# Cached attention and a Mish block on one core: the first and the last value loads cut differently, and half of the weights turned ahead of a wait

## The chip, the core and the metric

The kernel runs on one core of one Trainium2 chip. The core's engines are named as in the profile: PE (TensorE, matrix products), DVE (VectorE), ACT (ScalarE), POOL (GpSimd) and SP (SyncE, which here only issues loads). Sixteen DMA engines move data between the chip's memory and SBUF. The metric is the device time of one execution in microseconds (us); the time of a kernel is the median of its runs.

## The reference

One decode step, all in float32: 8 sequences, one new token each, model width 512.

- `xn = layernorm(x)`.
- Attention: `q = xn @ wq` gives 32 query heads of width 128. There are 8 key and value heads, each shared by 4 query heads, and a cache of 8192 positions: `scores = q k^T / sqrt(128)`, softmax over the 8192 positions, then the weighted sum of the values, then `@ wo`.
- A dense block: `h = xn @ w1 + b1` (1792 wide), `h * tanh(softplus(h))` (Mish), then `@ w2`.
- Result: `x + attention + dense block`, 8 x 512 numbers.

The key cache and the value cache hold 8 x 8 x 8192 x 128 numbers each, 268 MB each. Every number of them is used once, so some 561 MB pass from memory to the core in one execution.

## The kernel before, in words

**Units and packs.** The work on the caches is cut into 32 *units* (`UNITS`); a unit is two heads of one sequence: 8192 KB of keys (K0 to K31) and 8192 KB of values (V0 to V31). Two units make a *pack* (`PACKS` = 16), which share one softmax pass.

**Buffers.** SBUF has room for one unit of keys and one unit of values only. `kvb` (64 KB in each of 128 partitions) holds keys, `kva` (the same size) holds values, `kvw` (16 KB a partition) holds a quarter of `wq` or `wo`. At the beginning `kva` holds `w1`; at the end `kvb` holds the last unit's values and then `w2`.

**The loads** are all issued by SP, in the order of `early_loads` and `later_loads`, on one queue whose transfers land in order. A load that writes a buffer in use waits on SP until that buffer is told free, and everything behind it in the list waits with it. `k_free` is told by ACT when a unit's scores are done (line 729 of the program, `scalar_program`); `v_free` is told by DVE when a unit's values are done (`pass_on(s.valued, s.v_free)`), the first one when the products with `w1` are done; `w_free` is told by DVE in `keep_queries` and `add_outputs`. The order at the start is: wq0, K0, w1, wq1, K1, the first three quarters of V0 (semaphore `v0_in`), K2, the last quarter of V0 (`v_in`; it waits for `v0_in`), K3, wq2, V1, K4, V2, K5, wq3, V3, and so on, with a part of `wo` behind K9, K17 and K25. The order at the end is: K31, V29, the first 5/8 of V31 into `kvb` (`va_in`), V30, the last 3/8 of V31 (`vb_in`), then w2 in four parts (`w2a_in` to `w2d_in`) with the last part of `wo` behind the first. The first part of w2 waits for `w2_free`, told by PE when it has used the first 5 of 8 rounds of V31.

**PE** (`tensor_program`) runs a loop over n from -1 to 32. In step n it does the scores of unit n, on odd steps the sums that bring a pack's scores together (`rows`), sometimes a quarter of the queries (`queries`), then the values of unit n-2 (`values`, in 8 rounds over the buffer, `ROUNDS`), and on odd steps `merges`; `turn` and `outputs` follow when a head pair is complete. Ahead of the loop `turn_x` turns the normalised x twice: whole, for the queries, and, after POOL has sorted it (`x_split`), in eight parts for the products with `w1` (`mish_products`, in step 0). Behind the loop it does the end: the rest of V31, the early products with `w2` (`down_early`), `merges`, `turn`, `outputs`, and the rest of the products with `w2` (`down`), with `add_up` between them.

**ACT** copies scores out of PSUM and computes exponentials, in two halves of a pack's positions (`exponents(0)`, `exponents(1)`; the second half needs `exp_next`, which DVE tells when it has turned the first).

**DVE** (`vector_program`) does, for each pack: `expand` (it spreads the queries of a unit), `gather(0)` of the pack before, `maximum`, `expand`, then waits for the values of the pack's second predecessor unit (`valued`), passes that on as `v_free`, and does `gather(1)` and `collect`. Then it turns both halves of the exponentials (`turn_exponents`: a transpose and an addition) and writes them as weights into `pt` (`weights(c, b)`: half c, unit b of the pack, two additions each). `pt[:, 0]` is what PE reads; `pt[:, 1]` is copied over it when the first unit's values are done. When all is written DVE tells `p_is`, on which PE's values wait.

Of the kernel before, what the change touches and what calls it, by code (L numbers as in the profile page):

```python
# [13 lines left out]
P = 128  # L14
B = 8
D = 512
# [7 lines left out]
G = 4  # L24
# [3 lines left out]
BW = 1024  # L28
# [4 lines left out]
Q = P // G  # L33
# [68 lines left out]
def kernel(  # L102
# [18 lines left out]
    def bank(shape, name):  # L121
        return nc.alloc_psum_tensor(name, list(shape), F32).ap()

    names = (
        "x_in b1_in k_in v_in w_in w1_in v0_in va_in vb_in w2_free w2a_in w2b_in w2c_in w2d_in "
        "k_free v_free w_free q_free c_free scored copied_ex "
        "x_ready x_pool x_turned x_split x_split_turned x_is xw_is id_pe id_dve root rooted "
        "q_is rows_are max_is max_turned max_wide max_back shifts_are exp_done exp_next "
# [74 lines left out]
    def load(landed, dst, src, free=None, n=0):  # L203
        got = sp.dma_start(dst, src)
        if n:
            got.wait_op(free, n, "sem-ge")
        got.then_inc(landed, 16)
        return got
# [7 lines left out]
    def load_v(n):  # L216
        given["v"] += 1
        return load(s.v_in, kva, unit(v, n), s.v_free, given["v"])
# [5 lines left out]
    def load_wq(i):  # L224
        return load_w(wq[i * CC : (i + 1) * CC])
# [4 lines left out]
    w1_sb = kva[:, : W1R * F // 2]  # L230
    w2_sb = kvb[:, : W2N * D]
    W2_PARTS = ((0, 8), (8, 11), (11, 13), (13, 14))
    FIRST_V = 3 * KR * BW // 4
    LAST_ROUNDS = 5
    LAST_V = LAST_ROUNDS * KR * BW // ROUNDS

    def early_loads():
        first = [act.dma_start(x_sb, x), load_wq(0), act.dma_start(b1_sb, b1.rearrange("(g f) -> g f", g=G))]
# [6 lines left out]
    def later_loads():  # L245
        load_wq(1)
        load_k(1)
        first = unit(v, 0)
        given["v"] += 1
        load(s.v0_in, kva[:, :FIRST_V], first[:, :FIRST_V], s.v_free, given["v"])  # L250
        for n in range(2, UNITS):
            load_k(n)
            p, b = divmod(n, PB)
            if b == 1 and p in (1, 2):
                load_wq(p + 1)
            if b == 1 and p in (4, 8, 12):
                load_wo(p // 4 - 1)
            if n == 2:
                load(s.v_in, kva[:, FIRST_V:], first[:, FIRST_V:], s.v0_in, 16)
            else:  # L260
                load_v(n - 2)
        last = unit(v, UNITS - 1)
        load(s.va_in, kvb[:, :LAST_V], last[:, :LAST_V], s.k_free, given["k"])
        load_v(UNITS - 2)
        load(s.vb_in, kvb[:, LAST_V:], last[:, LAST_V:], s.k_free, given["k"])
        parts = list(zip(W2_PARTS, (s.w2a_in, s.w2b_in, s.w2c_in, s.w2d_in)))
        for (lo, hi), landed in parts:
            cols = slice(lo * D, hi * D)
            load(landed, w2_sb[:, cols], rows_of(w2)[:, cols], s.w2_free, 1)
            if lo == 0:  # L270
                load_wo(PAIRS - 1)

    def pool_setup():
        scratch = pt.rearrange("p b c m t e h -> p (b c m t e h)")
# [24 lines left out]
        pool.close()  # L299

    def normalise():
        dve.memset(xnT, 0.0)
# [79 lines left out]

    def turn_x():
        scratch = pt.rearrange("p b c m t e h -> p (b c m t e h)")
        xc, xs = scratch[:B, :D], scratch[:B, 2 * D : 2 * D + W1R * P]
# [4 lines left out]
        last.then_inc(s.x_turned, 1)  # L390
        take(pe, s.x_split)
        for r in range(W1R):
            last = pe.transpose(O[:, r * B : (r + 1) * B], xs[:, r * P : (r + 1) * P], ident[:B, :B])
        last.then_inc(s.x_split_turned, 1)
# [312 lines left out]
    def add_up():  # L707

        for g in range(G):
            pe.matmul(X[Q * g : Q * g + B, :P], rsel[:, :B], acc[:, g * P : (g + 1) * P], start=False, stop=False)  # L710

    def part(e, value):

        return e.If_eq(e.to_reg(value), 0)
# [27 lines left out]
    def vector_program():  # L742
# [8 lines left out]
        with e.Fori(0, PACKS) as p:  # L751
            dve.take(s.q_free)
            expand(2 * p + 1)
            dve.close()
            with part(e, (p - 1) & 16):
                dve.pass_on(s.valued, s.v_free)
                gather(0)
                dve.tensor_copy(
                    pt[:, 0].rearrange("p c m t e h -> p (c m t e h)"),
                    pt[:, 1].rearrange("p c m t e h -> p (c m t e h)"),  # L760
                )
                dve.tell(s.p_is)
                dve.close()
            e.end_ifs()
            maximum()
            dve.take(s.q_free)
            expand((2 * p + 2) & (UNITS - 1))
            dve.close()
            with part(e, (p - 1) & 16):
                dve.pass_on(s.valued, s.v_free)  # L770
                gather(1)
                dve.tell(s.o_is)
                collect((p - 1) & (NP - 1))
                dve.close()
            e.end_ifs()
            with part(e, (p - 4) & 19):
                keep_turned()
                dve.close()
            e.end_ifs()
            turn_exponents(0)  # L780
            weights(0, 0)
            weights(0, 1)
            turn_exponents(1)
            weights(1, 0)
            weights(1, 1)
            row_sums()
# [23 lines left out]
    def tensor_program():  # L810
        turn_x()
        with pe.Fori(-1, UNITS + 1) as n:
            with part(pe, n & 32):
                scores()
            pe.end_ifs()
            with part(pe, n):
                mish_products()
            pe.end_ifs()
            with part(pe, (n - 1) & 33):
# [91 lines left out]
```

## Time and profile before

| | |
|---|---|
| time, median of 3 runs | 1317.35 us (1316.45 to 1317.71) |
| the profiled execution's own time | 1317.75 us |
| its span, first to last instruction | 1316.4 us |
| busy: PE, DVE, ACT | 705.9, 386.6, 146.1 us |
| moved by DMA | 561.17 MB, mean 426 GB/s |
| mean granted clock of PE | 0.761 |

The profile is one execution. Busy times overlap, since the engines run side by side; a wait is shown as idle time in front of an instruction, with what ended it (PEq or DVEq is the engine's own sequencer, waiting for a semaphore). Line 72 (`L72`) is the helper through which all of DVE's and POOL's work is recorded, so their rows are told apart by tiles: `os` is a gather, `raw<-wide` a turning of exponentials, `pt<-raw` weights, `wide<-h` the first operation of `keep_queries`, `qT<-qc` an expansion. Line 204 is the helper that issues loads. On PE, L449 is scores, L540 values, L393 the transposes of the sorted x, L563 merges, L581 turn, L608 outputs. In a timeline row the columns are start, duration, engine, line, operation, written and read tiles with shapes, count, and in brackets the idle time ahead of it. In a row of stretches the columns are the stretch, its length, the busy time of PE, PEld (weight loads of PE), DVE, ACT and POOL with the count of instructions, the granted clock of PE, the DMA engines' busy share and GB/s.

### The profile page before, as it was taken

How to read it: one execution, taken by the hardware profiler on the slowest of the kernel's cores; microseconds unless marked ns; L12 is line 12 of the kernel's file. 1: busy time of each engine (PE TensorE's matmuls, PEld its weight loads, DVE VectorE, ACT ScalarE, POOL GpSimd, SP SyncE). 2: the span in 40 equal slices, each digit the busy share in tenths (PEclk: the TensorE clock that was granted, in tenths of full speed). 3: DMA queues.
4: the chain of work that ended last, by engine and by line, in shares of the span. 5: the costliest groups of instructions: out<-in, count | busy, mean ns of one | idle time of the engine just before them, and what ended most of it. 6: DMA issues, size and time to landing. Idle time of an engine off the chain costs nothing. (4 is left out here: it accounts for less than half of the span.)

```text
span 1316.4 us, 16643 instructions
## 1 busy us (share of the span) xinstructions
PE 705.9 (54%) x6808; PEld 226.2 (17%) x6808; DVE 386.6 (29%) x613; ACT 146.1 (11%) x339; POOL 4.9 (0%) x10
## 2 busy tenths in 40 slices
PE   3455745536546455646545555554744645554637
PEld 1111211212112111211112111111211211111112
DVE  4442151512315032141501414041141412304051
ACT  0020110101111020110201111010111101111010
POOL 0000000000000000000000000000000000000000
PEclk9777968768778777877768677777867768777768
DMA  9997999999999999999999999999999999999997
GB/s 401 423 425 317 460 414 446 414 446 446 414 446 414 446 446 414 446 416 444 446 414 446 416 444 446 414 446 420 440 446 414 446 420 440 446 414 446 432 426 307
DMA packets 11551, 561.17 MB, mean 426 GB/s; under 512 B 1292, under 2 KB 1424, under 8 KB 1816
## 3 DMA queue, kind: packets, MB, share of 16 engines
q1 hardware_dynamic: 11520, 561.06, 98.8%
q8 instruction: 4, 0.07, 0.0%
q10 hardware_dynamic: 24, 0.02, 0.0%
q14 instruction: 3, 0.02, 0.0%
HBM read 561.01 MB, written 0.07 MB: 426 GB/s over the span
## 5 line engine op out<-in xcount | busy, mean ns | idle before, releaser
L449 PE MATMUL c<-kvb,qT 64*32 64x512 f32 x4096 | 288.8, 723 | 283.1 <-PEq L98 283.1
L540 PE MATMUL o<-kva,pt 128*32 128x512 f32 x1984 | 275.4, 717 | 190.1 <-PEq L98 190.1
L449 PEld LDWEIGHTS c<-kvb,qT 64*32 64x32 f32 x4096 | 87.9, 127 | 479.4 <-issue 479.4
L540 PEld LDWEIGHTS o<-kva,pt 128*32 128x32 f32 x1984 | 77.9, 129 | 376.6 <-issue 376.6
L72 DVE TENSOR_SCALAR os<-o,isel 128x128 f32<-128x128 f32 x31 | 10.9, 351 | 434.9 <-DVEq L98 434.9
L72 DVE STREAM_TRANSPOSE raw<-wide 128x2048 f32<-128x2048 f32 x36 | 126.0, 3501 | 11.3 <-DVEq L98 10.7
L498 ACT ACTIVATE wide<-s,nms 128x512 f32<-128x512 f32 x128 | 86.2, 685 | 384.3 <-ACTq L98 384.3
L72 DVE TENSOR_REDUCE nm<-s 128x1 f32<-128x1024 f32 x16 | 19.6, 1225 | 356.2 <-DVEq L98 356.2
L733 ACT COPY sc<-c 128x512 f32<-128x512 f32 x64 | 34.4, 589 | 566.0 <-ACTq L98 565.9
L465 PE MATMUL s<-sc,csel 64*128 64x512 f32 x256 | 59.3, 602 | 24.0 <-ACT sc L733 24.0
L72 DVE TENSOR_TENSOR pt<-raw 64x256 f32<-64x256 f32 x128 | 53.7, 419 | 4.2
L72 DVE TENSOR_TENSOR raw<-raw 128x1024 f32<-128x1024 f32 x32 | 39.2, 1226 | 2.9
L733 ACT ACT_TABLE_LOAD x16 | 20.5, 1283 | 169.3 <-ACTq L98 169.3
L465 PEld LDWEIGHTS s<-sc,csel 64*128 64x128 f32 x256 | 23.4, 186 | 61.1 <-ACT sc L733 38.5
L72 DVE SCALAR_TENSOR_TENSOR os<-o,isel,os 128x128 f32<-128x128 f32 x93 | 32.6, 351 | 3.3
L72 DVE TENSOR_TENSOR qT<-qc,bsel 128x512 f32<-128x512 f32 x33 | 22.9, 693 | 28.4 <-DVEq L98 26.1
L563 PE MATMUL x<-hsel,os 128*128 128x8 f32 x64 | 9.9, 263 | 30.2 <-PEq L98 30.2
L498 ACT ACTIVATION_READ_ACCUMULATOR wide<-s,nms 128x1 f32 x128 | 26.0, 203 | 0.0
L402 PE MATMUL h<-kvw,xnT 128*64 128x512 f32 x64 | 22.7, 854 | 3.0 <-PEq L98 1.8
L540 PE MATMUL c<-kvb,pt 128*32 128x512 f32 x64 | 9.7, 763 | 15.3 <-PEq L98 15.3
L474 PE MATMUL m<-ident,nm 128*1 128x128 f32 x16 | 4.3, 269 | 24.6 <-PEq L98 24.6
L608 PE MATMUL h<-kvw,oW 128*8 128x512 f32 x64 | 14.2, 1036 | 5.9 <-PEq L98 5.9
(99 smaller groups left out, 154.4 us busy)
## 6 DMA issues: line engine op xcount, KB each, us to landing
kvw<-in_wq SPq DMA_DIRECT2D x4, 2048.0 KB, 22.8
kvw<-in_wo SPq DMA_DIRECT2D x4, 2048.0 KB, 33.1
kva<-in_v SPq DMA_DIRECT2D x1, 6144.0 KB, 34.1
kvb<-in_v SPq DMA_DIRECT2D x1, 5120.0 KB, 21.7
kva<-in_w SPq DMA_DIRECT2D x1, 3584.0 KB, 36.2
kvb<-in_v SPq DMA_DIRECT2D x1, 3072.0 KB, 28.8
kva<-in_v SPq DMA_DIRECT2D x1, 2048.0 KB, 24.9
kvb<-in_w SPq DMA_DIRECT2D x1, 2048.0 KB, 9.0
```

The costliest lines, as they stand in the source:

```text
L72: got = getattr(self.e, method)(*args, **kw)
L402: last = pe.matmul(H[HE * e : HE * (e + 1), :], xnT[:, r].rearrange("p g q -> p (g q)"), kvw[:, r * BW + e * D : r * BW + (e + 1) * D], st ...
L449: last = pe.matmul(C[e][Q * g : Q * (g + 1), :], t[rows, r], kvb[rows, r * BW + c * 512 : r * BW + (c + 1) * 512], start=(r < 2), stop=(r ...
L465: last = pe.matmul(S[:, c * 512 : (c + 1) * 512], csel[half_of, b, e].rearrange("p u b h -> p (u b h)"), sc[b][e][half_of, :], start=(b == ...
L474: pe.transpose(M[:1, 0:P], nm, ident).then_inc(s.max_turned, 1)
L498: last = act.activation(ex[:, :, k, :], S[:, c * 512 : (c + 1) * 512].rearrange("p (t f) -> p t f", t=HT), AF.Exp, bias=nms[:, k : k + 1], ...
L540: last = pe.matmul(to[Q * c : Q * (c + 1), :], pt[:, b, j % 2, j // 2].rearrange("p t e h -> p (t e h)"), vt[:, W4 * DH * j : W4 * DH * (j ...
L563: pe.matmul(X[:, at : at + 2 * REP], os[b], hsel, start=True, stop=True)
L608: last = pe.matmul(H[Q * r : Q * r + B, :], oW[:, r, h, :], kvw[:, at : at + D], start=(start and h == 0), stop=(h == 1))
L733: last = act.copy(sc[b][e], C[e])
```

## The change

1. *First values.* The first part of V0 is 5/8 of the unit, not 3/4; the second part is 3/8. The load of wq2 moves from behind K3 to directly behind the second part of V0, ahead of K3. (wq3 stays behind K5.)
2. *The last two units of values.* The first part of V31 is 11/16 of the unit, the second 5/16; PE still uses 5 of 8 rounds of it at first. V30 is loaded in two parts, the first 6 of 8 rounds (`v_in`) and the last 2 (`v2_in`). PE's `values` in the loop is cut in the same way for every unit, with a take of one credit (`v_more`) between the cuts. POOL gives 30 credits at the start, and the 31st when V30's second part has landed.
3. *Weights.* DVE turns the first half of the exponentials and writes `weights(0, 1)` ahead of its wait for `valued`, and `weights(0, 0)` behind it as before.
4. *split_x.* The eight transposes of the sorted x leave `turn_x` and stand in step 0 of PE's loop, behind the scores of unit 0 and ahead of `mish_products`.
5. *fill.* Behind the last `merges` and behind the last `turn`, PE does four products whose result nobody reads (into the scores' bank).

```diff
-    FIRST_V = 3 * KR * BW // 4
+    FIRST_V = 5 * KR * BW // 8
+    EARLY_ROUNDS = 6
+    EARLY_V = EARLY_ROUNDS * KR * BW // ROUNDS
     LAST_ROUNDS = 5
-    LAST_V = LAST_ROUNDS * KR * BW // ROUNDS
+    LAST_V = 11 * KR * BW // 16
...
         for n in range(2, UNITS):
             load_k(n)
             p, b = divmod(n, PB)
-            if b == 1 and p in (1, 2):
-                load_wq(p + 1)
+            if n == 2:
+                load(s.v_in, kva[:, FIRST_V:], first[:, FIRST_V:], s.v0_in, 16)
+            if n in (2, 5):
+                load_wq(n // 2 + 1)
             if b == 1 and p in (4, 8, 12):
                 load_wo(p // 4 - 1)
-            if n == 2:
-                load(s.v_in, kva[:, FIRST_V:], first[:, FIRST_V:], s.v0_in, 16)
-            else:
+            if n > 2:
                 load_v(n - 2)
...
         load(s.va_in, kvb[:, :LAST_V], last[:, :LAST_V], s.k_free, given["k"])
-        load_v(UNITS - 2)
+        given["v"] += 1
+        load(s.v_in, kva[:, :EARLY_V], early[:, :EARLY_V], s.v_free, given["v"])
+        load(s.v2_in, kva[:, EARLY_V:], early[:, EARLY_V:], s.v_free, given["v"])
         load(s.vb_in, kvb[:, LAST_V:], last[:, LAST_V:], s.k_free, given["k"])
...
         pool.close()
+        nc.gpsimd.wait_ge(s.v2_in, 0).then_inc(s.v_more, UNITS - 2)
+        nc.gpsimd.wait_ge(s.v2_in, 16).then_inc(s.v_more, 1)
...
         last.then_inc(s.x_turned, 1)
+
+    def split_x():
...
         take(pe, s.x_split)
         for r in range(W1R):
             last = pe.transpose(O[:, r * B : (r + 1) * B], xs[:, r * P : (r + 1) * P], ident[:B, :B])
...
+    def fill():
+
+        for c in range(G):
+            pe.matmul(S[Q * c : Q * (c + 1), :512], ones[:, :Q], sc[0][0], start=True, stop=True)
...
             expand((2 * p + 2) & (UNITS - 1))
             dve.close()
+            turn_exponents(0)
+            weights(0, 1)
+            dve.close()
             with part(e, (p - 1) & 16):
                 dve.pass_on(s.valued, s.v_free)
                 gather(1)
...
-            turn_exponents(0)
             weights(0, 0)
-            weights(0, 1)
             turn_exponents(1)
...
             with part(pe, n):
+                split_x()
                 mish_products()
...
                 take(pe, s.v_in, 16)
                 take(pe, s.p_is)
-                values(kva).then_inc(s.valued, 1)
+                values(kva, hi=EARLY_ROUNDS)
+                take(pe, s.v_more)
+                values(kva, lo=EARLY_ROUNDS).then_inc(s.valued, 1)
...
         merges()
+        fill()
         turn()
+        fill()
         outputs(start=False).then_inc(s.h_done, 1)
```

More of the change, by code (lines that the diff above doesn't have):

```diff
@@ L124 @@
     names = (
-        "x_in b1_in k_in v_in w_in w1_in v0_in va_in vb_in w2_free w2a_in w2b_in w2c_in w2d_in "
+        "x_in b1_in k_in v_in w_in w1_in v0_in v2_in v_more va_in vb_in w2_free w2a_in w2b_in w2c_in w2d_in "
         "k_free v_free w_free q_free c_free scored copied_ex "
@@ L253, in later_loads @@
             p, b = divmod(n, PB)
-            if b == 1 and p in (1, 2):
-                load_wq(p + 1)
+            if n == 2:
+                load(s.v_in, kva[:, FIRST_V:], first[:, FIRST_V:], s.v0_in, 16)
+            if n in (2, 5):
+                load_wq(n // 2 + 1)
             if b == 1 and p in (4, 8, 12):
                 load_wo(p // 4 - 1)
-            if n == 2:
-                load(s.v_in, kva[:, FIRST_V:], first[:, FIRST_V:], s.v0_in, 16)
-            else:
+            if n > 2:
                 load_v(n - 2)
-        last = unit(v, UNITS - 1)
+        last, early = unit(v, UNITS - 1), unit(v, UNITS - 2)
         load(s.va_in, kvb[:, :LAST_V], last[:, :LAST_V], s.k_free, given["k"])
-        load_v(UNITS - 2)
+        given["v"] += 1
+        load(s.v_in, kva[:, :EARLY_V], early[:, :EARLY_V], s.v_free, given["v"])
+        load(s.v2_in, kva[:, EARLY_V:], early[:, EARLY_V:], s.v_free, given["v"])
         load(s.vb_in, kvb[:, LAST_V:], last[:, LAST_V:], s.k_free, given["k"])
@@ L384, in turn_x @@
         scratch = pt.rearrange("p b c m t e h -> p (b c m t e h)")
-        xc, xs = scratch[:B, :D], scratch[:B, 2 * D : 2 * D + W1R * P]
+        xc = scratch[:B, :D]
         take(pe, s.id_pe)
@@ L390, in turn_x @@
         last.then_inc(s.x_turned, 1)
+    def split_x():
+        scratch = pt.rearrange("p b c m t e h -> p (b c m t e h)")
+        xs = scratch[:B, 2 * D : 2 * D + W1R * P]
         take(pe, s.x_split)
```

## The prediction

> **What bounds the kernel now.** I read the page first (busy shares, then the slices), then stretches of the DMA engines, then the issue times on SP's queue with each load's time to landing, and last the end of the timeline.
>
> ```profile
> span 1316.4 us, 16643 instructions
> PE 705.9 (54%) x6808; PEld 226.2 (17%) x6808; DVE 386.6 (29%) x613; ACT 146.1 (11%) x339; POOL 4.9 (0%) x10
> DMA  9997999999999999999999999999999999999997
> ...
> 96.00:112.00 16.00, 14.35 (x176) 4.68 (x180) 7.89 (x13) 2.36 (x3) 0.00 (x0) 0.81 0.57 223
> 120.00:660.00 540.00, 293.01 (x2848) 93.88 (x2848) 156.67 (x236) 63.00 (x147) 0.00 (x0) 0.76 1.00 433
> ...
> kvb<-in_kT SPq DMA_DIRECT2D x32, 29.1
> ```
>
> No engine is busy over 54%, while the DMA engines are full except in the fourth and the last slice. From 120 to 660 us they move 433 GB/s, from 96 to 112 only 223. So the loads are the bound: the time is the bytes at that rate plus the holes, plus what follows the last landing. Between 96 and 112 us (433-223)/433 x 16 = 7.8 us is lost. Here are the rows of that hole: SP's issues first, then the landings of the loads issued at 72.44, 76.60, 106.82, 107.19 and 114.39, in that order (the last column is us from issue to landing).
>
> ```profile
> 72.44 0.33 SPq L204 DMA_DIRECT2D kvb<-in_kT  x1
> 76.60 0.33 SPq L204 DMA_DIRECT2D kva<-in_v  x1
> 106.82 0.33 SPq L204 DMA_DIRECT2D kvb<-in_kT  x1
> 107.19 0.43 SPq L204 DMA_DIRECT2D kvw<-in_wq  x1
> 114.39 0.33 SPq L204 DMA_DIRECT2D kva<-in_v  x1
> ...
> kvb<-in_kT SPq DMA_DIRECT2D x1, 24.2
> kva<-in_v SPq DMA_DIRECT2D x1, 2048.0 KB, 24.9
> kvb<-in_kT SPq DMA_DIRECT2D x1, 21.7
> kvw<-in_wq SPq DMA_DIRECT2D x1, 2048.0 KB, 26.3
> kva<-in_v SPq DMA_DIRECT2D x1, 38.4
> ...
> 97.11 9.56 PE L449 MATMUL c<-kvb,qT 64*32 64x512 f32 x128 [11.15 <-PEq L98]
> 98.69 2.48 DVE L72 TENSOR_SCALAR wide<-h 128x512 f32<-128x512 f32 x4 [0.76 <-DVEq L98]
> ```
>
> Issue plus time to landing: K2 lands at 96.64, the last quarter of V0 at 101.50, K3 at 128.52, wq2 at 133.49, V1 at 152.79. The quarter took 101.50-96.64 = 4.86 us for 2048 KB (2.43 per 1024 KB, 19.44 for a whole 8192 KB unit). K3 took 27.02 behind it, 7.6 too many: its buffer is free only when scores(2) end at 106.67, and nothing else was queued. Issued into an empty queue, K3 needed 21.7, so starting costs 2.3 us. I take the bubble before a load as 2.3 minus its lead (its issue against the landing before it), if that is positive. The usual lead is 29.1 minus 19.4, about 10 us.
>
> **The change, part by part.**
>
> *First values and wq2.* The first part of V0 was 6144 KB and landed at 76.6 (SP issues the rest at 76.60, on that landing); with 5120 KB it lands 2.43 earlier, 74.2. K2 is issued at 72.44 as now: lead 1.8, bubble 0.5. As K2 took 20.0 even with a lead of 4.2 (96.64-76.6), I give it 20.1: K2 at 94.3. The rest of V0, 3072 KB at 2.43, lands at 101.6. wq2 now stands ahead of K3 on SP and waits for `w_free`, which DVE tells just before the row at 98.69; K3 queues behind that wait. Lead 2.9, no bubble: wq2 lands at 101.6+4.87 (the row's 133.49-128.52 is 4.97; a pro-rated 4.86) = 106.5. Scores(2) start 0.47 after K2 lands (97.11-96.64), run 9.56, and K3 is issued 10.2 after that landing, at 104.5; lead 2.0, a bubble of 0.3, which I raise to 0.6 for K2's unexplained 0.6. K3 lands at 106.5+19.44+0.6 = 126.5, and V1, now directly behind, 19.3 later (152.79-133.49) at 145.8. **Gain 152.8-145.8 = 7.0 us.** Bounds: 8.2 with no bubble at K2 or K3; 5.5 if each costs 0.75 more. The cover that wq2 gave K4 is gone (it stood between K3 and V1): K4 is issued at 126.5+10.2 = 136.7, 9 us ahead of V1's landing, the usual lead, so nothing. wq3 keeps its place.
>
> *split_x moved behind scores(0).*
>
> ```profile
> 13.34 0.99 PE L393 MATMUL o<-ident,pt 8*128 8x8 f32 x8 [1.96 <-PEq L98]
> 58.52 0.69 DVE L72 TENSOR_TENSOR qT<-qc,bsel 128x512 f32<-128x512 f32 x1 [0.53 <-DVEq L98]
> 62.48 9.81 PE L449 MATMUL c<-kvb,qT 64*32 64x512 f32 x128 [17.96 <-PEq L98]
> ```
>
> Queries(0) start some 3 us earlier, but scores(0) wait for K0's landing too, so I count on none of it beyond 0.8. Behind scores(0) stand the eight transposes (0.99), two hops and xw on DVE, 1.7 to 2 us in all, before the first products. Net, the mish chain and the expansion at its end (58.52) come about 1 us later, done at 60.2 instead of 59.2; scores(1) start at 62.48 on K1's landing. Cost nothing, cover 2 us; past it each us lands on K2's issue, one for one.
>
> *Weights half turned early.*
>
> ```profile
> L498 ACT ACTIVATE wide<-s,nms 128x512 f32<-128x512 f32 x128 | 86.2, 685 | 384.3 <-ACTq L98 384.3
> ...
> 636.54 0.35 DVE L72 TENSOR_SCALAR os<-o,isel 128x128 f32<-128x128 f32 x1 [8.92 <-DVEq L98]
> ...
> 1270.82 3.60 DVE L72 STREAM_TRANSPOSE raw<-wide 128x2048 f32<-128x2048 f32 x1 [0.61 <-DVEq L98]
> 1275.83 1.78 DVE L72 TENSOR_TENSOR pt<-raw 64x256 f32<-64x256 f32 x4
> ```
>
> Moved ahead of the wait on `valued`: transpose, add and half the weights, 5.01+0.89 = 5.9 us. The first four exponentials take 4 x 0.685 = 2.74 us, the expansion runs beside 0.69 of them, so DVE has 2.1 to wait and comes to `valued` 8.0 us after the expansion. It waits there 8.92 us now in the shortest case (636.54), so that wait still ends last; queued behind it are `v_free` and the gather. In the loop this gains nothing: loads pace it. The credit's take on PE lies inside values, in front of a lead of 10 us; bounded by 0 and 0.82 us a unit (PE's idle time before the row at 1304.88 below), nothing on the path.
>
> *The tail.* The landings of V30, va, vb and w2a, then the timeline; V31 lies in kvb, its first part is va, its second vb.
>
> ```profile
> kva<-in_v SPq DMA_DIRECT2D x1, 21.9
> kvb<-in_v SPq DMA_DIRECT2D x1, 5120.0 KB, 21.7
> kvb<-in_v SPq DMA_DIRECT2D x1, 3072.0 KB, 28.8
> kvb<-in_w SPq DMA_DIRECT2D x1, 2048.0 KB, 9.0
> ...
> 1246.90 0.33 SPq L204 DMA_DIRECT2D kvb<-in_v  x1
> 1266.89 0.33 SPq L204 DMA_DIRECT2D kva<-in_v  x1
> 1284.94 6.98 PE L540 MATMUL c<-kvb,pt 128*32 128x512 f32 x40 [15.35 <-PEq L98]
> 1291.73 7.05 PE L540 MATMUL o<-kva,pt 128*32 128x512 f32 x64
> 1291.97 0.33 SPq L204 DMA_DIRECT2D kvb<-in_w  x1
> 1298.59 2.76 PE L540 MATMUL c<-kvb,pt 128*32 128x512 f32 x24
> 1303.25 0.58 PE L563 MATMUL x<-hsel,os 128*128 128x8 f32 x4 [0.17 <-PEq L98]
> 1304.88 1.08 PE L581 MATMUL x<-oT,tid 128*128 128x64 f32 x8 [0.82 <-PEq L98]
> 1307.43 3.38 PE L608 MATMUL h<-kvw,oW 128*8 128x512 f32 x16 [1.48 <-PEq L98]
> 1313.50 0.35 SPq L866 DMA_DIRECT2D out<-acc  x1
> 1307.00:1307.50 0.50, 0.07 (x4) 0.10 (x8) 0.08 (x1) 0.00 (x0) 0.00 (x0) 0.55 1.12 459
> ```
>
> From the weights at 1284.94 PE runs nearly without a gap to 1303: 6.98, 7.05, 2.76 us of values, then w2a's products. In times of the old run: va landed at 1268.60; with 512 KB more it lands at 1269.8; V30's issue at 1266.89 then has a lead of 2.9 instead of 1.7, and its old excess (1288.79-1268.60-19.44 = 0.75) should go; V30a at 1284.4, V30b 1289.3, vb (2560 KB, 6.1) 1295.4, w2a (4.9, from 1300.97-1296.07) 1300.25 instead of 1300.97. Weights 5.9 earlier: va's values 1279.05 to 1286.0 (w2a is issued then, in good time), V30's to 1293.1 with V30b long there, a wait for vb, its values to 1298.2, gather(1) to 1299.9 (four operations of 0.35 as at 636.54, and a hop), and w2a's products from its landing, 1300.3. Merges stood 2.28 behind that landing, some 0.2 of it values' end. So what is late next is w2a, and merges start at 1302.35, only 0.9 before the old 1303.25.
>
> One fill is a round of values, 7.05/8 = 0.88. The first lies in the 0.82 between merges and turn (turn 0.06 late, 1304.05), the second in the 1.48 before outputs, now at 1306.6. There the granted clock fell (0.55 at 1307.0, 1.00 before), and outputs' 16 products took 3.38 where two rounds of warm values take 1.76. If the fills keep the clock, h is done 1.6 sooner; the rest as now (1313.50-1307.43 = 6.07 from outputs to the last issue, less 1.6), and the output leaves at 1311.05 instead of 1313.50: 2.45. If V30's excess stays, w2a lands 0.72 later: 1.75. **I take 2.1**; bounds 0.1 and 2.8.
>
> Two rules of the Trainium skill bear on this. In "DMA: Bandwidth & Descriptors", section "Anatomy of one DMA", each DMA has a fixed cost of about 2.0 us; charged for V30's second part, the sum would be 7.1 instead of 9.1. The trace agrees only for an empty queue: the quarter of V0, queued 20 us ahead, paid none. In "TensorE: Matmul & The Clock Gate", section "The HAM clock gate", the clock halves after an idle window of about 3.4 us; by that rule outputs were warm already and the fills bring nothing, so the tail would give 0.9 and the sum 7.9. The trace differs, since it fell with no gap on PE longer than 1.48.
>
> **Sum:** 7.0 + 2.1 = 9.1. The profiled execution took 1317.75 (its span 1316.4 and 1.35 around it), 0.4 above the median of 1317.35. 1317.75-9.1 = 1308.65, less that 0.4: 1308.3.
>
> **Rivals.** *The tail gives nothing* (1310.4 = 1317.35-7.0). PE now has two waits of about 2.2 us (for vb, for w2a); the row at 1307 shows that the clock falls in a stretch of little work without a long gap. If it falls there, merges come later by up to 1.5, each fill takes 1.76 instead of 0.88, and the 2.1 is spent. For it: that row. Against: the products between the waits are wide ones.
>
> *The hole stays* (1315.2 = 1317.35-2.1): wq2 would have to be issued no sooner than about 107, if DVE told `w_free` 8 us later, or K2 moved by as much. Nothing in DVE's first pass grows by more than tenths. A half of it (scores(1) late by 3 us through the mish chain) gives 1311.8.
>
> *Slower:* the early turning stands ahead of `v_free` on DVE once a pack, in 15 packs. If it came 7.7 us later than I reckon (the 0.9 us of slack at 636.54, then a lead of 9.1 less 2.3), every second V load would open a bubble; from 8.5 us on, 0.8 x 15 = 12 us outweigh the gain, for example 1320.3. Against it: the moved instructions' times are measured and fixed.
>
> **How the numbers follow.** Forecast 0.62 (own range 1306.3 to 1309.6: bounds 8.2+2.8 and 6.3+1.4), tail nothing 0.20, half the hole 0.06, hole stays 0.06, slower 0.06. The first two hold 0.82, so the range is 1306.3 to 1311.3 (1310.4, and 0.9 less from the hole). About 0.2%, 2.6 us, can be told from no change: faster 0.88, same 0.06, slower 0.06.
>
> **What would show it.** DMA between 96 and 112 us near 430 GB/s; wq2 issued near 98.7, K3 near 104.5, V1 landing near 145.8. Every later issue 7 us earlier. In the tail, relative to va's issue, weights 6 us sooner, w2a's landing ending PE's wait, outputs in 1.8 us at clock 1.00. Wrong if wq2's issue comes after 104, if scores(1) move past 63, or if outputs keep 3.4 us.

## The result, and the profile after

| | before | after |
|---|---|---|
| median | 1317.53 us (8 runs, 1314.80 to 1318.64) | 1308.82 us (8 runs, 1307.08 to 1313.27) |
| ratio, 95% interval | | 0.9939 (0.9927 to 0.9952) |
| profiled execution, its span | 1317.75, 1316.4 us | 1307.95, 1306.6 us |

The changed kernel is faster by 8.0 us by that ratio (6.3 to 9.6, as shares of 1317.5). Run again beside the last experiments it gave 0.9944 (0.9931 to 0.9958). The forecast was 1308.3.

The page of the changed kernel, its head and the 40 slices of DMA:

```profile
span 1306.6 us, 16725 instructions
PE 707.4 (54%) x6824; PEld 227.3 (17%) x6824; DVE 385.9 (30%) x613; ACT 146.1 (11%) x339; POOL 4.9 (0%) x10
DMA  9999999999999999999999999999999999999998
```

The fourth slice, 7 before, is 9 now; the engines' busy times are as they were. The stretch that held the hole (columns as before, the last is GB/s):

```profile
96.00:112.00 16.00, 14.04 (x184) 4.51 (x168) 8.92 (x16) 2.36 (x3) 0.00 (x0) 0.95 1.03 422
```

422 GB/s stand where 223 stood. SP's issues of the changed kernel: K2, the rest of V0, wq2, K3 and V1 around the old hole, then V31's first part and the output:

```profile
71.76 0.33 SPq L204 DMA_DIRECT2D kvb<-in_kT  x1
74.02 0.33 SPq L204 DMA_DIRECT2D kva<-in_v  x1
98.51 0.33 SPq L204 DMA_DIRECT2D kvw<-in_wq  x1
103.12 0.33 SPq L204 DMA_DIRECT2D kvb<-in_kT  x1
110.69 0.33 SPq L204 DMA_DIRECT2D kva<-in_v  x1
...
1240.00 0.33 SPq L204 DMA_DIRECT2D kvb<-in_v  x1
1305.02 0.35 SPq L887 DMA_DIRECT2D out<-acc  x1
```

And the time to landing of the loads issued at 98.51, 103.12 and 110.69:

```profile
kvw<-in_wq SPq DMA_DIRECT2D x1, 2048.0 KB, 8.1
kvb<-in_kT SPq DMA_DIRECT2D x1, 24.6
kva<-in_v SPq DMA_DIRECT2D x1, 36.4
```

wq2 lands at 106.61, K3 at 127.72, V1 at 147.09 (issue and time to landing added, here and in the tables below; V1 landed at 152.79 before). The end on PE, from the first weights of V31 to the outputs:

```profile
1271.80 6.12 PE L550 MATMUL c<-kvb,pt 128*32 128x512 f32 x40 [9.31 <-PEq L98]
1278.51 7.07 PE L550 MATMUL o<-kva,pt 128*32 128x512 f32 x64 [0.59 <-PEq L98]
1289.36 4.16 PE L550 MATMUL c<-kvb,pt 128*32 128x512 f32 x24 [3.77 <-PEq L98]
1294.25 1.90 PE L698 MATMUL h<-kvb,aT 128*8 128x512 f32 x16 [0.73 <-PEq L98]
1296.09 0.61 PE L573 MATMUL x<-hsel,os 128*128 128x8 f32 x4
1296.86 1.06 PE L725 MATMUL s<-sc,ones 128*32 128x512 f32 x8
1297.85 1.10 PE L591 MATMUL x<-oT,tid 128*128 128x64 f32 x8
1298.89 1.06 PE L725 MATMUL s<-sc,ones 128*32 128x512 f32 x8
1300.44 1.90 PE L618 MATMUL h<-kvw,oW 128*8 128x512 f32 x16 [0.49 <-PEq L98]
```

The two rows of L725 are the fills. Behind them the 16 products of the outputs take 1.90, where they took 3.38.

The 9.8 us between the two spans fall apart as follows. V1 lands 5.70 sooner (152.79 against 147.09). From V1's landing to V29's little changed: 1103.67 before, 1103.27 now, 0.40 less. From V29's landing (1256.46 and 1250.36) to the output's issue it was 57.04 and is 54.66, 2.38 less. The output itself took 2.9 us to land in the profile before and takes 1.6 now; that 1.3 belongs to one execution, since every other profile shows 1.5 or 1.6. Nor is all of the 2.38 the change's: with the first loads alone, where the program of the tail is the old one, the same stretch took 55.48 (below).

### The profile page after: what moved, and what is told of

Same layout as the page of the kernel before. It is cut to its first block, busy times and chain, and to the rows that moved or that the text cites. A ratio compares the mean times of both kernels' runs of the same rounds, so it can differ in the third digit from the quotient of the medians.

```text
span 1306.6 us, 16725 instructions
## 1 busy us (share of the span) xinstructions
PE 707.4 (54%) x6824; PEld 227.3 (17%) x6824; DVE 385.9 (30%) x613; ACT 146.1 (11%) x339; POOL 4.9 (0%) x10
## 5 line engine op out<-in xcount | busy, mean ns | idle before, releaser
L573 PEld LDWEIGHTS x<-hsel,os 128*128 128x128 f32 x64 | 9.4, 210 | 44.1 <-issue 44.1
```

What stands on the lines that cost most here:

```text
L573: pe.matmul(X[:, at : at + 2 * REP], os[b], hsel, start=True, stop=True)
```

## The experiments

The theory: moving wq2 closes the hole, the fills keep the clock of the end, and part 3 and V30's cut let PE run ahead of w2a. The rivals are those of the prediction: a tail that gives nothing, a hole closed only in part. Ratios are against the kernel before on the same chip; "us" is 1 less the ratio, times 1317. The last two columns are from the one profiled execution of each: V1's landing, and the time from V29's landing to the output's issue (57.04 before).

| kernel | median (runs) | ratio, 95% interval | us | V1 lands | V29 landing to output |
|---|---|---|---|---|---|
| after | 1308.82 (8) | 0.9939 (0.9927 to 0.9952) | 8.0 | 147.09 | 54.66 |
| after, again | 1308.31 (5) | 0.9944 (0.9931 to 0.9958) | 7.4 | 146.31 | 55.14 |
| first loads alone | 1311.41 (10) | 0.9957 (0.9944 to 0.9971) | 5.7 | 151.25 | 55.48 |
| all but the first loads | 1313.92 (10) | 0.9982 (0.9972 to 0.9991) | 2.4 | 151.05 | 55.12 |
| no fills | 1310.00 (4) | 0.9945 (0.9929 to 0.9962) | 7.2 | 148.47 | 57.05 |
| weights late | 1309.59 (4) | 0.9939 (0.9923 to 0.9956) | 8.0 | 150.51 | 55.06 |
| wq2 behind K3, 5/8 kept | 1314.88 (1) | | | 153.27 | 55.21 |
| 3/4, wq2 ahead | 1309.05 (1) | | | 147.22 | 55.50 |
| V30 in one load | 1310.90 (10) | 0.9959 (0.9945 to 0.9973) | 5.4 | 147.52 | 56.50 |
| products as fill | 1312.24 (5) | 0.9966 (0.9953 to 0.9979) | 4.5 | 150.23 | 56.98 |
| w_free earlier | 1309.05 (4) | 0.9936 (0.9912 to 0.9960) | 8.4 | 149.19 | 54.89 |
| warmed scores | 1315.63 (11) | 0.9992 (0.9982 to 1.0002) | 1.1 | 156.31 | 55.69 |
| warmed scores and end | 1315.87 (11) | 0.9988 (0.9979 to 0.9998) | 1.6 | 151.48 | 56.11 |

**First loads alone: part 1 put into the kernel before.**

```diff
-    FIRST_V = 3 * KR * BW // 4
+    FIRST_V = 5 * KR * BW // 8
...
-            if b == 1 and p in (1, 2):
-                load_wq(p + 1)
+            if n in (2, 5):
+                load_wq(n // 2 + 1)
```

> The kernel before with the change's first loads alone (5/8 and 3/8, wq2 ahead of K3). Theory of the sum: the two gains are separate and add. K3 is issued near 103 to 104.5, V1 lands near 147 (it does in the changed kernel, forecast 145.8), and the tail is as before, 38.0 us from va's issue to PE's products on it and outputs 3.4 us long: gain 5.7 to 7.0, time 1310.4 to 1311.7. Rival, the hole is everything: the tail parts bring nothing, so this kernel is as fast as the changed one, 1308.8.

It gave 5.7 us (3.8 to 7.4), the lower end of what was expected. **All but the first loads**: the changed kernel with the old order and cut at the start.

```diff
-    FIRST_V = 5 * KR * BW // 8
+    FIRST_V = 3 * KR * BW // 4
...
-            if n in (2, 5):
-                load_wq(n // 2 + 1)
+            if b == 1 and p in (1, 2):
+                load_wq(p + 1)
```

> The changed kernel with the first loads put back (3/4 and 1/4, wq2 behind K3). Theory of the sum: the hole is back, K3 is issued near 106.8 and V1 lands near 152.8; from va's issue to the output's issue it takes 65 us as in the changed kernel against 66.6 before: gain 2 to 3, time 1314.5 to 1315.5. Rival, the hole is everything: 1317.5.

It gave 2.4 us (1.2 to 3.7), within the 2 to 3 that were expected. 5.7 and 2.4 make 8.1, and the whole change gives 8.0: within these intervals the two gains add up. They are not cleanly the start's and the tail's, though. The second kernel keeps split_x, and in its profile the first queries start at 13.15 instead of 15.26 and V1 lands at 151.05, 1.74 sooner than before. And with the first loads alone K3 was still issued late:

```profile
108.72 0.33 SPq L204 DMA_DIRECT2D kvb<-in_kT  x1
```

V1 landed at 151.25, where 147 was expected: 1.54 sooner than before. (This execution took 1313.28, 1.87 more than the median.) In that profile K1 and K2 were issued 2.15 and 2.11 us ahead of the landing before them, and landed 21.65 and 22.19 us behind it instead of some 19.4. That is the first sight of what kept the prediction's 7.0 from coming out (below). Its end did not keep the old times either; the outputs:

```profile
1304.51 2.79 PE L608 MATMUL h<-kvw,oW 128*8 128x512 f32 x16 [1.48 <-PEq L98]
```

V30 took 19.3 from landing to landing, without the excess of 0.75 that it paid in the profile before; the merges start 45.63 behind V29's landing (46.79 before, 45.73 in the changed kernel), and the outputs took 2.79 instead of 3.38. So 1.56 of the 2.38 above came without any of the tail's parts, and ahead of the merges no gain can be told from what executions differ by.

**Without the fills.**

```diff
         merges()
-        fill()
         turn()
-        fill()
         outputs(start=False).then_inc(s.h_done, 1)
```

> The changed kernel without the two fills. Theory of the fill: the clock falls before outputs, which take 3.4 us instead of 1.9; merges as in the changed kernel; time 1310.3. Rival by the Trainium skill (TensorE: Matmul & The Clock Gate, The HAM clock gate): no idle window of 3.4 us lies between w2a's products and outputs, the clock stays at 1.00 and outputs take 1.9 us, time 1308.8.

The end on PE without fills:

```profile
1296.37 1.90 PE L698 MATMUL h<-kvb,aT 128*8 128x512 f32 x16 [1.20 <-PEq L98]
1298.21 0.61 PE L573 MATMUL x<-hsel,os 128*128 128x8 f32 x4
1299.87 1.07 PE L591 MATMUL x<-oT,tid 128*128 128x64 f32 x8 [0.82 <-PEq L98]
1302.42 3.60 PE L618 MATMUL h<-kvw,oW 128*8 128x512 f32 x16 [1.48 <-PEq L98]
```

and its granted clock (the third number from the end) as the outputs begin:

```profile
1302.40:1302.90 0.50, 0.48 (x4) 0.15 (x8) 0.00 (x0) 0.00 (x0) 0.00 (x0) 0.50 0.37 143
```

The outputs are back at 3.60, the products behind them at 1.52 instead of 0.84. From V29's landing to the output it takes 57.05, all of the old time. Some 0.6 of that loss stands ahead of the merges, where w2a landed late; the rest is the fills': from the merges to the output's issue it takes 10.76 against 8.93. This last stretch took 8.91 to 8.98 in all nine profiles with the fills, and 9.88 (first loads alone), 10.25 (before) and 10.76 (here) in the three that have nothing in their place. So in the profiles the fills are worth 0.9 to 1.8 us. The medians show less of it: 0.9945 against 0.9939 or 0.9944, with intervals that cover each other. The 1.8 us that this profile shows is within what four runs leave open.

**Weights late: part 3 undone.**

```diff
             expand((2 * p + 2) & (UNITS - 1))
             dve.close()
-            turn_exponents(0)
-            weights(0, 1)
-            dve.close()
...
+            turn_exponents(0)
             weights(0, 0)
+            weights(0, 1)
```

> The changed kernel with the first half of the exponentials turned behind the wait again. Theory: the 6.2 us go mostly into waits, since PE now waits for vb (3.8) and w2a: products on va start 38.0 us behind va's issue instead of 31.8, no wait for vb is left, and merges come 0.5 to 1.0 later: time 1309.3 to 1309.8. Rival, the weights carry the tail: the end comes later by the greater part of the 6.2 us, 1312 to 1315.

PE's end with late weights:

```profile
1282.21 6.50 PE L550 MATMUL c<-kvb,pt 128*32 128x512 f32 x40 [15.35 <-PEq L98]
...
1295.39 2.76 PE L550 MATMUL c<-kvb,pt 128*32 128x512 f32 x24
...
1300.05 0.58 PE L573 MATMUL x<-hsel,os 128*128 128x8 f32 x4
```

The weights come 15.35 behind the work before them instead of 9.31, then PE runs with no wait for vb. Counted from the issue of V31's first part (1243.94 here, 1240.00 in the changed kernel) the merges start at 56.11 here and at 56.09 there, and the output leaves at 65.02 in both. The 6 us that the weights gain turn into 3.77 of waiting for vb, 0.73 for w2a, and 1.40 more for vb's products on a lower clock. With V30 cut, part 3 is worth nothing that shows; the ratio is the same 0.9939.

**V30 in one load, no credit.**

```diff
-        given["v"] += 1
-        load(s.v_in, kva[:, :EARLY_V], early[:, :EARLY_V], s.v_free, given["v"])
-        load(s.v2_in, kva[:, EARLY_V:], early[:, EARLY_V:], s.v_free, given["v"])
+        load_v(UNITS - 2)
...
-                values(kva, hi=EARLY_ROUNDS)
-                take(pe, s.v_more)
-                values(kva, lo=EARLY_ROUNDS).then_inc(s.valued, 1)
+                values(kva).then_inc(s.valued, 1)
```

> The changed kernel with V30 in one load and without the credit. Theory: the cut is worth nothing, since PE waits for vb behind V30's products in the changed kernel: the products on V30 start 5 us later, near 1283 in the changed kernel's times, end just behind vb's landing, and merges wait for w2a as before: 1308.8. Rival, the early start of V30 carries the tail: 1310 or more. Rival, the credit costs PE in each of 31 units: 1308 or less.

```profile
1273.75 6.01 PE L546 MATMUL c<-kvb,pt 128*32 128x512 f32 x40 [9.32 <-PEq L98]
1284.64 9.96 PE L546 MATMUL o<-kva,pt 128*32 128x512 f32 x64 [4.89 <-PEq L98]
1294.41 2.76 PE L546 MATMUL c<-kvb,pt 128*32 128x512 f32 x24
```

V30 lands as a whole at 1284.40 (issue 1261.20, 23.2 to landing). PE, early with its weights, waits 4.89 us for it, and the 64 products behind that wait take 9.96 instead of 7.07. That is 56.50 instead of 54.66 from V29's landing to the output, and 0.9959 in place of 0.9939 or 0.9944 (the intervals still overlap a little). The expectation's first rival, 1310 or more, came true. I had counted the cut as worth nothing but the tenths of V30's excess. It is worth some 2 us, once the weights come early: with part 3 and without the cut, PE is idle for V30 and then slow. The two together show no gain: the merges start 47.61 behind V29's landing with part 3 alone, 45.73 with both, and 45.63 with neither, in the profile of the first loads alone.

**The two parts of the first loads taken apart**: wq2 behind K3 with the 5/8 kept, and 3/4 with wq2 ahead.

```diff
-            if n in (2, 5):
-                load_wq(n // 2 + 1)
+            if b == 1 and p in (1, 2):
+                load_wq(p + 1)
...
```

> The changed kernel with wq2 behind K3 again; 5/8 and 3/8 stay. Theory: the first part's size only moves K2 and with it K3's issue forward by 2.4 us, the queue still runs dry: V0's rest lands near 101.3, K3 is issued near 104.2 and lands near 126, V1 near 150. Rival, the size closes the hole: V1 near 147.

```diff
-    FIRST_V = 5 * KR * BW // 8
+    FIRST_V = 3 * KR * BW // 4
```

> The changed kernel with 3/4 and 1/4; wq2 stays ahead of K3. Theory, a load that is issued only 2 to 3.5 us ahead of the landing before it lands 0.4 to 3.4 us late, one with a lead over 5 does not: K2 has a lead of 4 to 5.5 and pays at most 0.7, wq2 with 2.5 pays about 0.6, K3 has a lead of about 0 and pays 2.3 or more; V1 lands between 147.5 and 150. Rival, the forecast's rule (2.3 less the lead): K2 and wq2 pay nothing, K3 pays 2.3, V1 near 147.0.

K3's issue, and the stretch of the hole, with wq2 behind K3:

```profile
107.20 0.33 SPq L204 DMA_DIRECT2D kvb<-in_kT  x1
```

```profile
96.00:112.00 16.00, 14.41 (x172) 4.68 (x176) 9.22 (x14) 2.36 (x3) 0.00 (x0) 0.78 0.69 279
```

With wq2 behind K3 the hole is there (279 GB/s), V1 lands at 153.27, as before the change (150 was expected, but K2, issued 1.9 ahead, came 2.1 late), and the one run took 1314.88; the kernel before had a median of 1315.61 on that chip. With wq2 ahead and 3/4, V1 lands at 147.22, 0.13 from the changed kernel, and the one run took 1309.05. By these two runs wq2's move is the whole of part 1. The 5/8 brings nothing here: it has K2's buffer filled 1.8 us sooner, and K3 takes that back (it lands at 127.72 with 5/8, at 127.85 with 3/4). V1's landing misses the theory's 147.5 to 150 and is near the rival's 147.0, but the rival's rule does not hold load by load: wq2, issued 1.9 ahead, paid 1.1 where it gives 0.4. K3, issued only 0.5 ahead, paid 1.9, near the rule's 1.8, and hardly more than the 1.7 that it paid in the changed kernel with a lead of 3.5, where the rule gives nothing.

**Real products in place of the fills**: if any wide products keep the clock, the early products with w2, cut in two, would do it at no cost.

```diff
         take(pe, s.w2a_in, 16)
-        down_early(*W2_PARTS[0])
         merges()
-        fill()
+        down_early(0, 4)
         turn()
-        fill()
+        down_early(4, 8)
         outputs(start=False).then_inc(s.h_done, 1)
```

> The changed kernel with the early products with w2 in the place of the two fills, four ahead of turn and four behind it. Theory: the products keep the clock as well as the fills, merges follow gather(1) and not w2a's products, outputs are 1.9 us long and start 0.5 to 0.8 sooner: time 1308.0 to 1308.4. Rival, half the products in each gap are too little, the clock falls and outputs take 3.4: 1309.5.

```profile
1299.00 0.58 PE L573 MATMUL x<-hsel,os 128*128 128x8 f32 x4 [1.89 <-PEq L98]
1299.74 1.58 PE L698 MATMUL h<-kvb,aT 128*8 128x512 f32 x8
1301.25 1.97 PE L591 MATMUL x<-oT,tid 128*128 128x64 f32 x8
1304.82 2.95 PE L618 MATMUL h<-kvw,oW 128*8 128x512 f32 x16
```

The rival's mechanism was right, and the loss is larger than its 1309.5. With these products taken from behind vb's, PE stands 1.89 us ahead of the merges, the merges' products are small, and the clock falls in the first eight wide ones (1.58 instead of 1.06 for the same number in a fill): the turn takes 1.97 instead of 1.10, the outputs 2.95. It gave 4.5 us. In the changed kernel the 16 early products with w2 stand directly ahead of the merges and the fills 0.7 us behind them, so that PE is never long without wide work.

**w_free told earlier**: DVE tells it for the first packs directly behind `weights(0, 1)`, so that wq2 may queue long ahead of its turn; the first time, for wq1, it tells it ahead of the loop.

```diff
     def keep_queries(pair):
 
-        dve.pass_on(s.h_done, s.w_free)
         dve.take(s.h_done)
...
         normalise()
+        dve.pass_on(s.h_done, s.w_free)
         keep_queries(slice(0, B))
...
             turn_exponents(0)
             weights(0, 1)
             dve.close()
+            with e.If_lt(e.to_reg(p), 3):
+                dve.pass_on(s.h_done, s.w_free)
+            e.end_ifs()
```

> The changed kernel with w_free told some 9 us earlier, as soon as DVE has turned the first half. Theory, a short lead costs: wq2 is issued near 90 with a lead of 11 and lands 4.87 behind V0's rest instead of 5.5; K3, issued at the same time, still has a lead of 2 to 3 and still lands 0.5 to 3 late; V1 lands 0.6 earlier at most, time 1308.2 to 1308.8. Rival, K3 pays because wq2 was late in the queue: K3 takes 19.4 and V1 lands near 144.7, time 1306.4.

```profile
89.17 0.33 SPq L204 DMA_DIRECT2D kvw<-in_wq  x1
105.57 0.33 SPq L204 DMA_DIRECT2D kvb<-in_kT  x1
```

wq2 is queued 14.07 us ahead and lands 4.83 behind V0's rest, with no excess (5.49 in the changed kernel). But K2 (lead 2.42) took 22.08 and K3 (lead 2.50) took 21.70, V1 lands at 149.19, where the theory had it 0.6 sooner at most than in the changed kernel and the rival at 144.7, and the ratio, 0.9936, cannot be told from 0.9939. In this profile the longer lead cures the load that has it; the ones with a short lead pay.

**Warmed scores**: with that, unread products ahead of the scores of K0, K1 and K2, so that these run at full clock and K1, K2 and K3 are issued sooner.

```diff
+    def warm(rounds):
+
+        for _ in range(rounds):
+            for c in range(G):
+                pe.matmul(
+                    O[Q * c : Q * (c + 1), :],
+                    ident[:, :Q],
+                    ident.rearrange("p (o i) -> p o i", o=1).to_broadcast([P, 4, P]),
+                    start=True,
+                    stop=True,
+                )
...
                 mish_products()
+                warm(18)
             pe.end_ifs()
...
                 queries()
+            pe.end_ifs()
+            with part(pe, (n + 1) & 61):
+                warm(10)
```

> The changed kernel with w_free told early and with products nobody reads on PE in its waits ahead of scores 0, 1 and 2 (10, 18 and 10 rounds), so that these scores run at the full clock (about 7 us instead of 8.6 to 9.3). Theory, what is still lost at the start is a short lead: K1, K2 and K3 are issued about 2 us sooner, with leads of 4.5 to 6, and land 19.4 behind the landing before; V1 lands between 144 and 145 instead of 147.1 to 150.5, time 1305.5 to 1306.5. Rival, the excess has nothing to do with the lead: V1 lands at 146 to 149, time 1308 to 1309.

**Warmed scores and end**: the same, with the merges first and the early products with w2 for fills, and three fills in the wait for vb.

```diff
+        for _ in range(3):
+            fill()
...
-        down_early(*W2_PARTS[0])
         merges()
-        fill()
+        down_early(0, 4)
         turn()
-        fill()
+        down_early(4, 8)
```

> The same, and in the tail merges no longer wait for w2a: the early products with w2 stand in the place of the two fills, and three fills stand in the wait for vb. Theory: vb's products take 2.8 us instead of 4.2, merges come 1.5 us sooner, outputs then wait for wo, the output leaves about 1.1 us sooner behind va's issue: time 1 us below the kernel beside it, 1304.5 to 1305.5. Rival, the last landing (w2d) ends the tail: no gain over it.

Both lost nearly all of the gain; neither theory nor rival came true. PE's start with warmed scores:

```profile
27.07 6.23 PE L412 MATMUL h<-kvw,xnT 128*64 128x512 f32 x16 [15.22 <-PEq L98]
33.23 8.79 PE L730 MATMUL o<-ident 128*32 128x512 f32 x80
42.36 7.10 PE L458 MATMUL c<-kvb,qT 64*32 64x512 f32 x128 [0.34 <-PEq L98]
```

The scores do run faster, 7.10 against 8.60 in the changed kernel. But the first queries start at 27.07, where the changed kernel has them at 12.72 (behind an idle 1.33), and with them all that follows: K1 is issued at 49.59 instead of 38.32, 7.40 behind the landing before it, and V1 lands at 156.31. So what warming would be worth at the start isn't known; this way of doing it cost more. In the version with the end the three fills did keep the clock through the wait for vb, as meant, but the end was none the better: the merges start 1.09 sooner behind V29's landing than in the changed kernel (44.64), and the output is issued 11.52 behind them instead of 8.93.

```profile
1294.66 2.78 PE L549 MATMUL c<-kvb,pt 128*32 128x512 f32 x24 [1.48 <-PEq L98]
1299.33 0.58 PE L572 MATMUL x<-hsel,os 128*128 128x8 f32 x4 [1.89 <-PEq L98]
1304.80 3.30 PE L617 MATMUL h<-kvw,oW 128*8 128x512 f32 x16
```

vb's products take 2.78, not 4.16; then come the 1.89 of waiting and the small products again, and the outputs at 3.30. Last, **the changed kernel once more**, beside these, to see how far its profile repeats:

> The changed kernel itself, on the same chip as the two others, to compare them with: 1308 to 1309.5; V1 lands between 147 and 150.5, its spread from profile to profile comes from the loads with short leads.

1308.31, V1 at 146.31 (a little sooner than expected), 55.14 from V29's landing to the output. No version beat the changed kernel.

## Why the prediction was right

The time (1308.82 for 1308.3) and the sign were right, and so was the mechanism of the start. The gain by the ratio is 8.0, where 9.1 was added up. V1 landed 5.70 sooner where 7.0 was forecast, and in no profile before 146.31, so the start was taken too large. The tail's 2.38 came near the forecast 2.1 by luck in part: the fills are shown, but 1.56 of it stands in the profile of the first loads alone as well. The medians of the two halves, 5.7 and 2.4, leave this open, since their intervals hold 7.0 and 2.1 too.

**The hole.** K2's landing was forecast at 94.3 and came at 93.86, wq2's issue 98.7 and 98.51, wq2's landing 106.5 and 106.61, K3's issue 104.5 and 103.12. To there the chain held, and K3's issue came even sooner. K3 then landed at 127.72 instead of 126.5, V1 at 147.09 instead of 145.8. The step that failed is the bubble rule, 2.3 less the lead if positive. By it wq2 (lead 2.61) and K3 (lead 3.49) owed nothing, and K3 was given 0.6. wq2 took 5.49 instead of 4.87, K3 21.11 instead of 19.44: 0.6 and 1.7. The 5.70 lies just above the stated lower bound of this term, 5.5. That the second half of part 1, the 5/8, would carry something was implied by the 2.43 in the sum; it carries nothing in the one run without it.

**split_x.** Cost nothing, as forecast: the expansion was at 58.87 (58.52 before), the scores of K1 began at 62.33 on K1's landing. Queries(0) start 2.5 us sooner, and K1 was issued at 38.32 instead of 39.44. That gives K1 a lead of 4.20 instead of 3.24, a thing that I had left out and that, by the table below, may help.

**The weights in the loop.** The slack on DVE at `valued` was 0.9 at its shortest by the forecast, which took 8.92 for the shortest wait before. It was not: the first one was 6.73. The first row is that one, in the kernel before; the second is the shortest of the changed kernel:

```profile
114.57 0.35 DVE L72 TENSOR_SCALAR os<-o,isel 128x128 f32<-128x128 f32 x1 [6.73 <-DVEq L98]
1182.01 0.35 DVE L72 TENSOR_SCALAR os<-o,isel 128x128 f32<-128x128 f32 x1 [0.71 <-DVEq L98]
```

0.71 is left in the shortest case (5.30 in the first). No load of values in the loop lost its lead, and V1's landing to V29's took the same. The rival of a late `v_free` fell.

**The tail.** That w2a's landing comes late next was right: it lands at 1294.08, the products start at 1294.25, and the merges start 1.06 sooner behind V29's landing than before (45.73 against 46.79), where 0.9 was forecast. That this is the change's gain is not shown, since it is 45.63 with the first loads alone. The weights' 5.9 us (6.24 measured: 38.04 before, 31.80 after the issue of V31's first part) did not buy it in any case, as the kernel with late weights shows (46.15, and the same output). V30's cut is what PE needs as soon as the weights are early. The wait for vb was 3.77, not 2.2, and there the rival came true: the clock fell, as this stretch of the changed kernel shows,

```profile
1290.00:1290.50 0.50, 0.50 (x8) 0.23 (x4) 0.00 (x0) 0.00 (x0) 0.00 (x0) 0.50 1.07 459
```

and vb's 24 products took 4.16 instead of 2.76. It cost nothing, because w2a landed 0.73 after PE was through. The rival's mechanism was there, and its price was hidden by the very transfer that I had named as late next. V30's excess of 0.75 went, as forecast (its first part, 6144 KB, took 14.49, where 14.58 is its share), though it went with the first loads alone too.

**The fills** were right in mechanism and nearly in size: they fit into the gaps (0.82 and 1.48 without them), outputs went from 3.38 to 1.90 for a forecast of 1.76, and from the merges to the output's issue it takes 8.93 instead of 10.25, 1.32 less where 1.55 was forecast.

**The two rules cited.** In "DMA: Bandwidth & Descriptors" of the Trainium skill, section "Anatomy of one DMA", the fixed cost of about 2.0 us stands for DMAs that GpSimd issues. The loads here are issued by SP, so the prediction charged it where that section does not apply, and the traces show no such cost for queued loads. V30's second part and vb together took 11.05 us (landing to landing) for 4608 KB, where 2.43 per 1024 KB makes 10.94. In "TensorE: Matmul & The Clock Gate" of the Trainium skill, section "The HAM clock gate", the clock halves after an idle window of about 3.4 us. The wait of 3.77 agrees with it. In the end without fills the clock had fallen with no gap over 0.82 behind the last warm products with w2: the trace fits the rule only if products a few columns wide are counted as idle (last section), which is argued here and not tested by itself.

## What to carry to other kernels

Where a load waits for a buffer and leaves the queue empty, look for another load whose own buffer comes free sooner and put it ahead: here 2048 KB moved one place was worth all of part 1's gain, and cutting sizes nothing. By the loads below, count a load as free only if it is queued some 5 us ahead of its turn; with less, allow it up to 3.4 us. At the end of a kernel a few unread wide products between small ones can be cheaper than the small ones' falling clock, but they have to stand close behind wide work (here 0.7 us; eight that came 2.6 us behind it did not hold the clock). Work that ends sooner in front of a landing is worth nothing until that landing moves too.

## What the runs showed of the hardware that was not expected

**A short lead costs, and not always the same.** The loads of the old hole in kernels whose first loads are issued by the same rules; lead is the landing before less the issue, time is landing to landing. Unburdened, 8192 KB take 19.3 to 19.4 us and 2048 KB 4.85.

| kernel | K2: lead, time | wq2: lead, time | K3: lead, time | V1 lands |
|---|---|---|---|---|
| after, again | 2.24, 19.76 | 2.59, 5.51 | 3.54, 20.46 | 146.31 |
| after | 2.23, 19.87 | 2.61, 5.49 | 3.49, 21.11 | 147.09 |
| V30 in one load | 2.30, 19.60 | 2.37, 5.63 | 3.51, 19.99 | 147.52 |
| no fills | 1.96, 19.74 | 2.23, 5.47 | 3.14, 21.36 | 148.47 |
| products as fill | 1.94, 22.46 | 5.09, 5.11 | 2.45, 21.65 | 150.23 |
| weights late | 1.84, 22.76 | 6.17, 4.83 | 2.54, 21.96 | 150.51 |

Leads from 1.84 to 3.54 cost 0.2 to 3.4 us, the lead of 5.09 some 0.3, that of 6.17 nothing, and at nearly the same lead K2 took 19.74 once and 22.46 another time. K1 shows the same: over all profiles, leads of 3.2 to 4.2 went with 19.3 to 21.0 us. Apart from DVE's order in one and the cut of PE's products in another, these kernels differ only in the tail, so the program hardly sets this spread; it is of the size of the changed kernel's own (1307.08 to 1313.27). The lead alone does not set it either, as K3 with 0.5 us shows (21.3 us, in the kernel with 3/4). In the changed kernel the three loads were 2.7 us late in all. These are its stretches from K2's start on, and the whole from K1's landing to V1's:

```profile
74.00:80.00 6.00, 3.35 (x18) 1.29 (x16) 1.90 (x5) 0.00 (x0) 0.00 (x0) 1.00 0.81 350
80.00:146.00 66.00, 34.57 (x356) 11.35 (x358) 24.93 (x34) 9.28 (x22) 0.00 (x0) 0.79 1.00 427
62.00:147.00 85.00, 49.09 (x504) 16.24 (x506) 27.26 (x38) 11.36 (x27) 0.00 (x0) 0.80 1.00 423
```

At 433 GB/s the whole would have been 2.0 us shorter, and more than half of that falls into the six microseconds behind 74, where K2 starts. So the greater part of the lateness is DMA time lost. For the rest, it would fit that the 16 engines get out of step and that the slowest of them sets the landing; that is argued here, not shown.

**A longer program on PE started later.** With the added products the first queries stood still until 27.07 (24.39 in the version with the changed end), behind an idle 15.22 (13.01), though wq0 had landed and x was turned, as in the changed kernel, which began at 12.72. The page of the kernel with warmed scores has five packets of instructions (0.08 MB), where the changed kernel has four (0.07 MB). That PE waited for code which queued behind the first loads would explain it. But the number of packets alone does not set the start: the kernels without fills and with products as fill have three, and begin at 12.73 and 12.91. It was not tried with the same products at another place of the program, and stays open.

**The clock fell while PE worked, on small products.** These are the granted clocks (third from the end) of the kernel without fills, in half microseconds, where it falls:

```profile
1300.00:1300.50 0.50, 0.50 (x6) 0.50 (x6) 0.00 (x0) 0.00 (x0) 0.00 (x0) 1.00 1.00 414
1300.50:1301.00 0.50, 0.45 (x4) 0.31 (x3) 0.00 (x0) 0.00 (x0) 0.00 (x0) 0.82 1.07 438
1301.00:1301.50 0.50, 0.00 (x0) 0.00 (x0) 0.37 (x2) 0.00 (x0) 0.00 (x0) 0.50 1.02 418
```

Its last wide product ended at 1298.27 (1296.37 and 1.90). Merges and turn, 8 to 64 columns wide, ran between that and the fall, with no gap over 0.82. In the kernel before, the last wide product ended at 1303.08 and the clock was 0.55 in the half microsecond from 1307.0. So the clock went some 2.5 and 4 us behind the last wide product. With the first loads alone it went 5 us behind it, and the outputs, wide again, were already running for 0.9 us; in the changed kernel's wait for vb, with PE idle, it went some 3.2 us behind. That narrow products count as little as idling would fit, and is not tested by itself. Two times eight unread products of 512 columns, 2.1 us of work, kept it at 1.00.
